# DeltaNet and SwiGLU on one Trainium2 core: gate and value of the late chunks by 15 block products for 18

## The chip, the core and the metric

The kernel runs on one core of a Trainium2 chip. A core has five engines that run side by side, each in the order of its own queue: TensorE (PE in the profile, its weight loads PEld) multiplies matrices into PSUM, VectorE (DVE) does elementwise work and 32x32 transposes, ScalarE (ACT) applies functions and copies, GpSimd (POOL) does elementwise work in SBUF, and SyncE (SP) issues transfers. They wait for each other by semaphores. The metric is the device time of one launch in microseconds; smaller is better.

## The reference

Two blocks follow each other. The first is a delta rule: for each of 4 x 8 heads a 48x48 state is carried over 768 positions. The second is a feed-forward block on the result, with 3072 tokens of 384 numbers (8 heads x 48) and 1536 hidden ones.

```python
k_n = k / (np.linalg.norm(k, axis=-1, keepdims=True) + 1e-06)
for t in range(S):
    y[:, :, t] = q_t @ state
    v_old = state^T @ k_t
    state = state + beta_t * outer(k_t, v_t - v_old)
...
g = x @ w_gate
silu = g * (1.0 / (1.0 + np.exp(-g)))
val = x @ w_val
return (silu * val) @ w_out
```

All inputs and outputs are float32.

## The kernel before, in words

The 768 positions are cut into 12 chunks of 64; a chunk is 256 tokens of the feed-forward block (4 batches x 64 positions), held transposed as `x_ffn`, three row blocks of 128 by 256 tokens. Two chunks make a group, whose triangular systems are inverted together.

**Recurrence.** `advance(c)` takes chunk c through four steps, each a few bundles of 64 small matmuls with VectorE or ScalarE in between. Step 1: products of keys and queries with the state (L924 into bank pair `px`, L933 into `py`), and the values minus the first (L941). Step 2: the inverse applied (L963) and copied (L975). Step 3: the new state (L1031, L1040), the output y (L1019) and its three copies (L1076, L1078). Step 4: y transposed (L1092) and copied to `x_ffn` (L1098).

**Preparation.** Keys and queries of later chunks are transposed (`turned`, L494: one operation of VectorE for a chunk's keys, one for its queries) and multiplied (`gram_steps`, L521). `invert(g)` then inverts the systems of group g. It is a generator: transposes (L563), norms and a power on GpSimd (L826), 31 pairs of a multiplication and an addition for the forward substitution (L593, L599; on VectorE for group 1, on GpSimd from group 2 on), transposes back (L563, L858, L863) and four copies of ScalarE (L869). It yields a cost after each piece, and the word `WAIT` where time is to pass. `fill(n)` runs it until costs of n are spent or until a `WAIT`. `join(g)` completes the inverse by two bundles of matmuls (L887, L901) with a copy of ScalarE between; for group 1 the joins are `join_late` (L792, L804).

**The order.** The engines' orders are as written (`manual_schedule`). `point(c)` places the next step of `advance(c)`, or a step of preparation; `finish(c)` places all that are left.

**Chunks 0 and 1** run their gate and value plainly (`gate_val`, L1295) while the weights are loaded and converted, then their outputs (`output`, L1322), in the order (0,0), (0,1), (1,0), (1,1). In `output(1, 1)` VectorE also makes sums of weight blocks (`sums_of_w`, 24 operations of 128x256, up to 175 us), nine of which are stored to DRAM (`kept`). GpSimd's last work before it is a memset of the `qpad` tiles (L158) at 121.84 to 123.68.

**Chunks 2 to 11** work in three rounds (`gate_val_fast`). A round treats two pairs of hidden blocks, f1 and f2, for gate and value and both halves of the tokens. Plainly that is 12 products of a weight block pair with an x block; a scheme of sums of blocks (as in Strassen's method) does it with 11. One product is `product4`: four matmuls of a 128x128 weight block with 128 tokens, each of which shows as two records, all on line L1199. ScalarE copies partial results from one PSUM bank to another (L1212, L1255) or to SBUF (L1252), VectorE adds them (`plus`, L1366; `minus` is L1363), ScalarE takes the silu of the gate half of a bank (L1229), and VectorE multiplies it by the value half (L1234) into `h_f`. Three of the summed weights are streamed from DRAM in each round (L1226). Recurrence and preparation lie at points within the rounds, with calls of `fill`, 12 a chunk with those of the output.

**Output of these chunks** (`output_fast`) is seven products of six matmuls of 128x192 (L1405, twelve records a product) on sums of h made by VectorE.

PSUM has eight banks: four `ffn_banks`, and the pairs `px` and `py`. The function `product4` and the round's beginning are:

```python
def product4(p, w, moving, start=False):
    for u in range(4):
        nc.tensor.matmul(
            p[:, u], w(u), moving, start=start and u == 0, stop=True,
            skip_group_check=True,
        )
```

Of the kernel before, what the change touches and what calls it, by code (L numbers as in the profile page):

```python
# [20 lines left out]
def kernel(  # L21
# [42 lines left out]
    ffn_pool = ctx.enter_context(tc.tile_pool(name="ffn", bufs=2))  # L64
# [129 lines left out]
    wg_sb = const.tile([128, KT, DFF], FP32, name="wg_sb")  # L194
    wv_sb = const.tile([128, KT, DFF], FP32, name="wv_sb")
# [5 lines left out]
    for f0, m in ((0, 256), (256, 256), (512, 256), (768, 256), (1024, PIECE)):  # L201
        for t in range(KT):
            for dst, src in ((wg_sb, moe_w_gate), (wv_sb, moe_w_val)):
                pieces.append((dst, src, t, f0, m))
    N_HALF = sum(piece[4] < PIECE for piece in pieces)
# [58 lines left out]
    def power_step(n):  # L264
        if n in powers or n not in staged:
# [7 lines left out]
            dst[:, t, f0 : f0 + m],  # L273
            words_of[:, :, 1].bitcast(FP32),
# [5 lines left out]
    def convert(ns, ahead=6):  # L280

        work_of = []
        for n in ns:
            dst, _, t, f0, m = pieces[n]
            power_step(n)
            place = staged.pop(n)[:, 0:m]
            work_of.append((dst[:, t, f0 : f0 + m].bitcast(U32), place, powers.pop(n)))
# [59 lines left out]
    kt, qt, a_sb, a_of, p_sb, xts = {}, {}, {}, {}, {}, {}  # L347

# [563 lines left out]
    def advance(c):  # L912
# [169 lines left out]
        xts[c] = ffn_pool.tile([128, KT, TOK], FP32, name="x_ffn")  # L1082
# [38 lines left out]
    def w_s(n, c):  # L1121
        if n < 4:
            return units(hp[5 + n])
        return units(hp[10] if c == FAST else p_places[0][:, 0:512])

    def m5_of(c, r):
        early = c == FAST and r == 0
        return units(hp[13] if early else p_places[0][:, 512:1024])

    kept = {  # L1130
        (n, r): dram.tile([128, 4, 128], FP32, name=f"w_s{n}_{r}")
        for n in (1, 2, 4)
        for r in range(3)
    }
    x_t = const.tile([128, 3, 128], FP32, name="x_t")

    def w_pair(m, t, f):
        return (wg_sb, wv_sb)[m][:, t, 128 * f : 128 * f + 256].rearrange(
            "p (i n) -> p i n", i=2
        )  # L1140

    made_in = {
        0: {1: hp[6], 2: hp[7], 4: hp[10]},
        1: {1: hp[1], 2: hp[2], 4: hp[0]},
        2: {1: hp[12], 2: hp[13], 4: hp[8]},
    }

    def sum_of_w(n, r):

        f1, f2 = 2 * r, 2 * r + 6  # L1150
        for m in range(2):
            s1, s2, s4 = (units(made_in[r][k])[:, 2 * m : 2 * m + 2] for k in (1, 2, 4))
            if n == 1:
                plus(s1, w_pair(m, 0, f2), w_pair(m, 1, f2))
            elif n == 2:
                minus(s2, s1, w_pair(m, 0, f1))
            elif n == 4:
                minus(s4, w_pair(m, 1, f1), s2)
            else:
                minus(w_pair(m, 0, f2), w_pair(m, 0, f1), w_pair(m, 0, f2))  # L1160
        if n != 3:
            nc.sync.dma_start(out=kept[n, r], in_=units(made_in[r][n]))

    sums_at = {
        2: [(1, 1), (2, 1), (4, 1)],
        4: [(1, 2), (2, 2), (4, 2)],
        6: [(3, 1), (3, 2)],
        8: [(1, 0), (2, 0)],
        12: [(4, 0), (3, 0)],
    }  # L1170

    def sums_of_w(f):
        for job in sums_at.pop(f, ()):
            sum_of_w(*job)

    def sums_of_x(c):

        left, right = slice(0, 128), slice(128, 256)
        b1, b2 = xts[c][:, 0], xts[c][:, 1]
        minus(x_t[:, 0], b1[:, right], b1[:, left])  # L1180
        minus(x_t[:, 1], b2[:, right], x_t[:, 0])
        minus(b1[:, right], b2[:, right], b1[:, right])
        minus(x_t[:, 2], b2[:, left], x_t[:, 1])
# [8 lines left out]
    ROUNDS = 3  # L1192

    p_x, p_w, p_y, p_v = (units(bank) for bank in ffn_banks)
    tok = slice(0, 128), slice(128, 256)

    def product4(p, w, moving, start=False):
        for u in range(4):
            nc.tensor.matmul(  # L1199
                p[:, u], w(u), moving, start=start and u == 0, stop=True,  # L1200
                skip_group_check=True,
            )

    def plain(t, f):
        return lambda u: w_pair(u // 2, t, f)[:, u % 2]

    def summed_w(n, c):
        return lambda u: w_s(n, c)[:, u]

    def begin(c, r):  # L1210
        product4(p_x, plain(0, 2 * r), xts[c][:, 0, tok[0]], True)
        nc.scalar.copy(p_y, p_x)  # L1212
# [5 lines left out]
    def gate_val_fast(c, r, fill):  # L1218

        f1, f2 = 2 * r, 2 * r + 6  # L1220
        x, m5 = xts[c], m5_of(c, r)

        def next_sums(n):
            to = c + (r == ROUNDS - 1)
            if to < NCH:
                nc.sync.dma_start(out=w_s(n, to), in_=kept[n, (r + 1) % ROUNDS])  # L1226

        def silu(p, n):
            nc.scalar.activation(  # L1229
                sil[:, n].rearrange("p (i n) -> p i n", i=2), p[:, 0:2], ACTF.Silu  # L1230
            )

        def times(p, n, f, j):
            nc.vector.tensor_tensor(  # L1234
                out=h_of(c, f, j),
                in0=sil[:, n].rearrange("p (i n) -> p i n", i=2),
                in1=p[:, 2:4],
                op=ALU.mult,
            )

        more = 1.5 if (c, r) <= (FAST + 1, 0) else 0

        def combo_and_fill(n):
            if c == FAST:
                combos.pop(0)()
                n -= 1.9
            fill(n)

        for f in (f1, f2):
            new_h(c, f, f // 2)  # L1250
        product4(p_w, summed_w(1, c), x_t[:, 0], True)
        nc.scalar.copy(m5, p_w)  # L1252
        next_sums(1)
        product4(p_y, summed_w(2, c), x_t[:, 1])
        nc.scalar.copy(p_v, p_y)  # L1255
        next_sums(2)
        load_late()
        product4(p_x, plain(1, f1), x[:, 1, tok[0]])
        product4(p_x, plain(2, f1), x[:, 2, tok[0]])
        plus(p_y, p_y, m5)  # L1260
        product4(p_v, plain(0, f2), x[:, 0, tok[1]])
        silu(p_x, 0)
        fill(1)
        times(p_x, 0, f1, 0)
        plus(p_w, p_v, m5)
        point_and_fill(c + 1, 3.4 + more, fill)
        product4(p_y, summed_w(4, c), x[:, 1, tok[1]])
        next_sums(4)
        load_late()
        product4(p_y, plain(2, f1), x[:, 2, tok[1]])  # L1270
        silu(p_y, 1)
        times(p_y, 1, f1, 1)
        product4(p_w, plain(2, f2), x[:, 2, tok[1]])
        silu(p_w, 0)
        times(p_w, 0, f2, 1)
        product4(p_v, plain(1, f2), x_t[:, 2])
        product4(p_v, plain(2, f2), x[:, 2, tok[0]])
        silu(p_v, 1)
        sums_of_h(c, f2)
        times(p_v, 1, f2, 0)  # L1280
        if r < ROUNDS - 1:
            begin(c, r + 1)
        else:
            clear(0)
# [521 lines left out]
```

## Time and profile before

| what | value |
|---|---|
| median of 3 runs | 699.82 us (698.36 to 700.54) |
| the profiled execution's own time | 696.37 us |
| its span, first to last instruction | 694.7 us |
| TensorE busy | 681.7 us (98%) |
| VectorE busy | 411.2 us (59%) |
| ScalarE busy | 259.5 us (37%) |
| GpSimd busy | 192.3 us (28%) |
| mean granted clock of TensorE | 0.994 |
| chunk 2 begins | 172 us |
| records of gate and value, chunks 2 to 11 (L1199) | 2640 |

The profile is of one execution. Its page lists the busy time of each engine, the span in 40 slices, the DMA queues, the chain of work that ended last, and the costliest groups of instructions. A row of the groups names the line, the engine, the operation, what it writes and reads, how often it ran, then its busy time and the mean duration of one in ns, then the idle time of the engine ahead of it and what ended that. The answers of the trace show the same execution further: the chain in order of time (start, duration, what), the timeline (start, duration, engine, line, operation) and a table of busy times in stretches, whose last three columns are TensorE's granted clock, the busy share of the DMA engines and GB/s. Times in such answers count from the span's start.

### The profile page before, as it was taken

Reading aid. Unit: us, or ns where it says so; the run is one execution under the profiler, and the core shown is the slowest. Engines: PE = TensorE matmul, PEld = TensorE weight load, DVE = VectorE, ACT = ScalarE, POOL = GpSimd, SP = SyncE. Lnnn points to the kernel's source line nnn. Section 1 sums busy time; section 2 is a strip of 40 time slices with the busy share of each in tenths; the row PEclk is TensorE's granted clock in tenths of the full one; section 3 lists DMA queues with packets and bytes.
Section 4 is the critical chain, followed back from the end, with each engine's and each line's share of the span. In section 5 each row is a group of like instructions: output and inputs, shape, how many; then the busy total and the mean of one; then the engine's idle time right before and its main releaser. Section 6 shows DMA issues by size and latency. Waiting matters only on the chain.

```text
span 694.7 us, 25664 instructions
## 1 busy us (share of the span) xinstructions
PE 681.7 (98%) x11380; PEld 636.3 (92%) x11380; DVE 411.2 (59%) x856; ACT 259.5 (37%) x549; POOL 192.3 (28%) x310
## 2 busy tenths in 40 slices
PE   8899999999999999999999999999999999999997
PEld 4688888757999999999999999999999999999997
DVE  6886789798657755647446456455565345333342
ACT  4774876214442532344233244233143242142230
POOL 5010031106882128820038820328800000000000
PEclk9899999999999999999999999999999999999999
DMA  9578724017550621464423363233363221121210
GB/s 137 151 187 215 215 78 151 1 35 177 128 111 14 116 79 40 105 119 79 93 72 70 74 134 70 56 84 72 67 119 70 56 63 46 55 63 46 69 47 23
DMA packets 143854, 62.31 MB, mean 90 GB/s; under 512 B 122976, under 2 KB 126048, under 8 KB 143744
## 3 DMA queue, kind: packets, MB, share of 16 engines
q1 hardware_dynamic: 141536, 60.19, 37.1%
q8 instruction: 89, 1.46, 0.9%
q10 hardware_dynamic: 2080, 0.39, 0.4%
q0 software_dynamic: 128, 0.10, 0.1%
q14 instruction: 21, 0.17, 0.1%
HBM read 53.58 MB, written 7.08 MB: 87 GB/s over the span
## 4 chain that ended last, share of the span: by engine, by line
PE 96%; ACT 2%; issue 1%; DVE 1%; DVEq 0%; ACTq 0%
PE ffn L1199 43%; PE ffn L1405 20%; PE ffn L1295 9%; PE ffn L1322 4%; PE p_px L963 2%; PE p_px L924 2%; PE p_py L933 2%; PE p_px L1031 1%; PE p_py L521 1%; PE p_py L1019 1%; PE p_px L521 1%; PE p_py L1092 1%; PE ffn L983 1%; PE p_px L645 1%; PE p_px L983 1%
## 5 line engine op out<-in xcount | busy, mean ns | idle before, releaser
L1199 PE MATMUL ffn<-x_ffn,wg_sb 128*128 128x128 f32 x840 | 128.2, 275 | 0.2 <-ACT x_ffn L1098 0.2
L1199 PE MATMUL ffn<-x_ffn,wv_sb 128*128 128x128 f32 x840 | 128.1, 275 | 0.0
L1199 PEld LDWEIGHTS ffn<-x_ffn,wg_sb 128*128 128x128 f32 x840 | 111.1, 192 | 0.3 <-ACT x_ffn L1098 0.3
L1199 PEld LDWEIGHTS ffn<-x_ffn,wv_sb 128*128 128x128 f32 x840 | 110.7, 192 | 0.0
L1234 DVE TENSOR_TENSOR h_f<-sil,ffn 128x256 f32<-128x256 f32 x120 | 49.9, 417 | 78.2 <-ACT sil L1229 76.4
L1229 ACT ACTIVATE sil<-ffn 128x256 f32<-128x256 f32 x120 | 46.1, 384 | 132.5 <-PE ffn L1199 130.8
L1405 PE MATMUL ffn<-wo_sb,h_f 128*128 128x192 f32 x480 | 83.4, 327 | 0.0
L826 POOL TENSOR_TENSOR n_b<-mb,half 128x32 f32<-128x32 f32 x5 | 30.0, 6003 | 183.3 <-DVE mb L563 183.3
L1366 DVE TENSOR_TENSOR ffn<-ffn,p_sb 128x512 f32<-128x512 f32 x58 | 40.5, 698 | 64.1 <-ACT ffn L1255 62.8
L1405 PEld LDWEIGHTS ffn<-wo_sb,h_f 128*128 128x128 f32 x480 | 78.1, 190 | 0.4
L599 POOL TENSOR_TENSOR zb<-zb,tmp 128x31 f32<-128x31 f32 (+15 forms) x124 | 71.4, 576 | 9.7
L593 POOL TENSOR_TENSOR tmp<-zb,mb 128x31 f32<-128x31 f32 (+15 forms) x124 | 67.0, 541 | 16.0 <-DVE mb L580 6.6
L1199 PE MATMUL ffn<-x_t,h_f 128*128 128x128 f32 x480 | 61.0, 280 | 0.2 <-ACT ffn L1212 0.2
L1199 PEld LDWEIGHTS ffn<-x_t,h_f 128*128 128x128 f32 x480 | 56.2, 191 | 1.4 <-ACT ffn L1212 0.4
L1366 DVE TENSOR_TENSOR o_sb<-o_sb,ffn 128x192 f32<-128x192 f32 x49 | 17.2, 352 | 61.9 <-PE ffn L1405 60.7
L1212 ACT COPY ffn<-ffn 128x512 f32<-128x512 f32 x30 | 17.1, 571 | 63.9 <-PE ffn L1199 63.9
L1405 PE MATMUL ffn<-last_k,h_f 128*128 128x192 f32 x200 | 35.9, 327 | 0.0
L1363 DVE TENSOR_TENSOR h_f<-h_f,h_f 128x256 f32<-128x256 f32 x60 | 30.2, 512 | 9.2 <-PE ffn L1405 8.2
L1295 PE MATMUL ffn<-x_ffn,wg_sb 128*128 128x256 f32 x144 | 34.4, 385 | 0.0
L1295 PE MATMUL ffn<-x_ffn,wv_sb 128*128 128x256 f32 x144 | 33.8, 382 | 0.0
L1405 PEld LDWEIGHTS ffn<-last_k,h_f 128*128 128x128 f32 x200 | 32.9, 190 | 0.0
L1295 PEld LDWEIGHTS ffn<-x_ffn,wg_sb 128*128 128x128 f32 x144 | 26.5, 190 | 4.4 <-DVE wg_sb L309 0.8
(304 smaller groups left out, 1100.2 us busy)
## 6 DMA issues: line engine op xcount, KB each, us to landing
h_f<-w_s SPq DMA_DIRECT2D x60, 256.0 KB, 2.8
p_sb<-w_s SPq DMA_DIRECT2D x27, 256.0 KB, 2.6
vin<-in_v_dram SPq DMA_DIRECT2D x48, 96.0 KB, 3.1
out_dram<-o_sb SPq DMA_DIRECT2D x48, 96.0 KB, 2.2
kn<-in_k_dram SPq DMA_DIRECT2D x20, 192.0 KB, 4.5
zt<-in_moe_w_out_dram SPq DMA_DIRECT2D x6, 384.0 KB, 3.6
qpad<-in_q_dram SPq DMA_DIRECT2D x36, 64.0 KB, 3.3
w_s<-h_f SPq DMA_DIRECT2D x7, 256.0 KB, 4.0
```

What stands on the lines that cost most here:

```text
L593: engine.tensor_tensor(out=t_v, in0=zb[:, 0 : j + 1, j : j + 1].to_broadcast([128, j + 1, m]), in1=mb[:, j : j + 1, j + 1 : R].to_broadcas ...
L599: engine.tensor_tensor(out=zb[:, 0 : j + 1, j + 1 : R], in0=zb[:, 0 : j + 1, j + 1 : R], in1=t_v, op=ALU.add,)
L826: nc.gpsimd.tensor_tensor(out=n, in0=mb.rearrange("p j i -> p (j i)")[:, 0 : R * R : R + 1], in1=half, op=ALU.pow,)
L1199: nc.tensor.matmul(p[:, u], w(u), moving, start=start and u == 0, stop=True, skip_group_check=True,)
L1212: nc.scalar.copy(p_y, p_x)
L1229: nc.scalar.activation(sil[:, n].rearrange("p (i n) -> p i n", i=2), p[:, 0:2], ACTF.Silu)
L1234: nc.vector.tensor_tensor(out=h_of(c, f, j), in0=sil[:, n].rearrange("p (i n) -> p i n", i=2), in1=p[:, 2:4], op=ALU.mult,)
L1295: nc.tensor.matmul(ps[name][:, i], w_sb[:, t, (f + i) * 128 : (f + i + 1) * 128], xts[c][:, t], start=(t == 0 and i == 0), stop=(t == KT - 1),
L1322: nc.tensor.matmul(p_o, hs[c, f - f % 2][:, f % 2, bp * 128 : (bp + 1) * 128], wo_sb[:, f], start=(f == 0), stop=(f == FT - 1),)
L1363: nc.vector.tensor_tensor(out=out, in0=a, in1=b, op=ALU.subtract)
L1366: nc.vector.tensor_tensor(out=out, in0=a, in1=b, op=ALU.add)
L1405: nc.tensor.matmul(p[x, part], a(f - f % 2)[:, f % 2], b(f), start=not begun and f == 0, stop=f == FH - 1, skip_group_check=True,)
```

## The change

Chunks 2 to 11 work in two halves instead of three rounds. A half (`r`) treats three pairs of hidden blocks, `PAIRS[r]`, for gate and value and both token halves: plainly 18 products, here 15. The order of its products and of the work on their banks is a list, `STEPS`, written out for both halves: `P` is a product into a bank (with a start flag where it is 1), `C` a copy from a bank to another with or without a minus sign, `T` a copy to an SBUF tile, `A` an addition or subtraction of such a tile, `S` a silu, `M` the multiplication. Five banks are used: the four `ffn_banks` (0 is `ffn2`, 1 `ffn3`, 2 `ffn0`, 4 `ffn1`) and the second bank of `px` (3).

VectorE makes ten sums of x blocks a chunk (`X_SUMS`, 128x128 each) instead of four operations. Gate and value weights move to one tile `w_all`, so that a pair's gate and value blocks lie together, 512 wide. The weight sums (`W_SUMS`, 16 for each half, 128x512 each) are made once by GpSimd, issued in the outputs of chunks 0 and 1 by `w_step`, many of them in place; six a half are stored to DRAM and streamed in each chunk through three tiles (`STREAM`, 12 loads a chunk for nine).

The steps of `advance(c + 1)` and the preparation move from the rounds into `output_fast`: `visit` places a step of the recurrence, and first completes the inverse and the joins that it needs; `prep_turn`, `prep_gram` and `prep_join` place the parts of the preparation. Within the halves remain two calls of `fill(1)` (after the first and the seventh operation of VectorE in the first half; in chunk 2 the sums of output weights instead), late loads, possible joins, and sums of h. Two calls of `fill` stand at the end of an output. Chunk 3's keys and queries and the last two joins of group 1 are placed ahead of chunk 2.

```diff
+    X_SUMS = (
+        (6, 0, 1, 1, -1), (7, 4, 1, 6, -1), (8, 5, 1, 7, -1),
...
+    W_SUMS = (
+        (9, 1, 1, 2, 1), (1, 2, 1, 5, 1), (10, 6, 1, 1, 1),
...
+    STREAM = (-1, -1, 5, 3, 1, -1, 4, 0, -1, 2, -1, -1, -1, -1, -1)
+    PAIRS = ((3, 1, 0), (2, 5, 4))
+    STEPS = (
+        ("P", 2, 10, 1),
+        ("P", 3, 7, 1),
+        ("C", 2, 0, -1),
+        ("P", 4, 5, 1),
+        ("P", 0, 4, 0),
...
+        ("T", 1, 1, 0),
+        ("A", 4, 1, 1),
+        ("P", 1, 11, 0),
+        ("S", 3, 2, 0),
+        ("P", 4, 2, 0),
+        ("M", 3, 2, 0),
+        ("S", 1, 0, 0),
+        ("M", 1, 0, 0),
+        ("T", 4, 0, 0),
+        ("S", 4, 1, 0),
+        ("A", 2, 0, 1),
+        ("S", 2, 4, 0),
+        ("M", 4, 1, 0),
+        ("M", 2, 4, 0),
+    )
...
-    def gate_val_fast(c, r, fill):
+    def gate_val_fast(c, r, behind):
+        for kind, a, b, s in STEPS:
+            bank = g_banks[a]
+            if kind == "P":
+                i = STREAM[b]
+                w = streams[i % 3] if i >= 0 else w_home(r, W_OF[b])
+                product4(bank, w, x_place(X_OF[b]), s > 0)
+                if i >= 0:
+                    load_stream(c, r, i + 3)
...
@@ def output(c, bp, fill, between=())
             if f in between:
                 fill(2)
                 point(2)
-                if (c, bp) == (1, 1):
-                    sums_of_w(f)
+            w_step(W_PACE)
...
+    def visit(c, fill):
+        n = c + 1
+        if n == NCH:
+            return
+        while not may_advance(n):
+            fill_some(1000)
+            prep_step(c)
+        step("advance", advance, n)
...
@@ def output_fast(c, fill)
+        visit(c, fill)
+        for f in (2, 4):
+            first_sums(c, f)
+        product_1()
         if c > FAST:
             clear(1)
+            visit(c, fill)
+            for f in (2, 4):
+                last_sum(c, f)
             product_2()
+            plus(o[0][:, right], o[0][:, right], p[0, 1])
+            visit(c, fill)
+            prep_turn(c)
             product_3()
             plus(o[1][:, right], o[0][:, right], p[1, 0])
+            visit(c, fill)
+            x_sums(c + 1)
             product_4()
+            prep_gram()
...
@@ the loop over chunks
         for c in range(2, NCH):
+            some = [lambda: fill(1)]
...
+                (0, "D", 1): some,
+                (0, "D", 7): some,
...
+            for r in range(2):
+                gate_val_fast(c, r, behind)
             output_fast(c, fill)
-            finish(c + 1)
-            x_sums(c + 1)
```

## The prediction

> **What bounds the kernel now.** I read four views: busy shares and chain, the chain in order of time, the groups, then timelines.
>
> ```profile
> PE 681.7 (98%) x11380; PEld 636.3 (92%) x11380; DVE 411.2 (59%) x856; ACT 259.5 (37%) x549; POOL 192.3 (28%) x310
> ...
> PE 96%; ACT 2%; issue 1%; DVE 1%; DVEq 0%; ACTq 0%
> ```
>
> TensorE is the chain, and from 174 us on it has almost no hole. So work taken off it is a gain, and each new wait of it is a loss. The chain in order of time prices both kinds of work in chunk 11, where nothing is mixed in:
>
> ```profile
> 647.36 29.57 PE ffn L1199 x264
> 676.93 13.67 PE ffn L1405 x84
> ```
>
> 264 records are 33 block products of eight: 0.896 us a product. One of the seven output products is 13.67/7 = 1.95 us. The groups (last number ahead of the second bar: mean ns) price what hangs behind TensorE:
>
> ```profile
> L1234 DVE TENSOR_TENSOR h_f<-sil,ffn 128x256 f32<-128x256 f32 x120 | 49.9, 417 | 78.2 <-ACT sil L1229 76.4
> ...
> L1366 DVE TENSOR_TENSOR ffn<-ffn,p_sb 128x512 f32<-128x512 f32 x58 | 40.5, 698 | 64.1 <-ACT ffn L1255 62.8
> ...
> L1252 ACT COPY p_sb<-ffn 128x512 f32<-128x512 f32 x29 | 17.0, 586 | 24.5 <-PE ffn L1199 24.2
> ...
> L563 DVE STREAM_TRANSPOSE zt<-zb 128x512 f32<-128x512 f32 x8 | 9.6, 1202 | 0.0
> ...
> L869 ACT COPY zt<-zt 32x512 f32<-32x512 f32 x16 | 9.2, 610 | 0.1
> ...
> L863 DVE STREAM_TRANSPOSE z<-zt 32x256 f32<-32x256 f32 x16 | 6.1, 415 | 0.2
> ```
>
> A silu (L1229) is 0.38 us. The timeline gives the hand-overs: the load after a product starts at 395.27, the silu of that product at 395.58 (0.31 us), its multiplication 0.04 us after the silu's end; ScalarE to TensorE takes 0.05 us (174.20 to 174.25). Last, GpSimd beside VectorE, and the join that waits for the inverse of group 1:
>
> ```profile
> 154.52 0.75 PE L792 MATMUL p_px<-zt,a_sb 32*32 32x32 f32 x64
> ...
> 279.70 0.64 POOL L593 TENSOR_TENSOR tmp<-zb,mb 128x256 f32<-128x256 f32 x1
> 279.73 0.76 DVE L1363 TENSOR_TENSOR x_t<-x_ffn 128x128 f32<-128x128 f32 x1
> 280.42 0.73 POOL L599 TENSOR_TENSOR zb<-zb,tmp 128x256 f32<-128x256 f32 x1
> 280.52 0.77 DVE L1363 TENSOR_TENSOR x_t<-x_ffn,x_t 128x128 f32<-128x128 f32 x1
> ...
> 438.74 0.28 DVE L1363 TENSOR_TENSOR x_t<-x_ffn 128x128 f32<-128x128 f32 x1
> ```
>
> The same subtraction takes 0.28 us alone and 0.76 beside GpSimd: each time it ends 0.15 us after GpSimd's operation does (280.34 and 280.49; 281.15 and 281.29). It stood still until GpSimd was through.
>
> **The change, part by part.**
>
> *Products.* 30 for 33 in each of ten chunks: 30 x 0.896 = 26.9 us less. There is no other saving: TensorE's other work stays.
>
> *Between the two halves of a chunk.* After the last product (P 4,2) bank 2 still waits for T 4, A 2, S 2 and M 2, and the next half opens with P 2,10 into that bank. TensorE takes its queue in order. 0.31 + 0.59 (copy) + 0.03 + 0.70 (sum) + 0.03 + 0.38 (silu) + 0.03 + 0.42 (product) + 0.05 = 2.54 us idle; ten times, 25.4. Before, the next round's first bank had been read long ago. Inside a half I walked all 15 products at 0.896: the copies end 0.02 to 0.07 us late at four places, 0.2 us a half. Bounds over 20 halves: 0 (hand-overs a little quicker) and 10 (0.3 more where a fill of 1.2 us stands ahead of A 4,1); I take 2.
>
> *Into the output.* The same tail covers bank 2, where product 1 begins. The first step of the recurrence stands between (L924 and L933, 1.08 + 0.93 us): 0.55 us is left, for chunks 2, 4, 6, 8, 10: 2.7. Chunk 11 has no recurrence: 2.5. Further on I find no wait: each of the four steps has a product of 1.95 us behind it against 0.95 (subtraction) or 1.43 (three y copies); the ten sums of x at 0.28 end some 6 us before they are read. The clears (0.33) and all the sums of h keep ahead of their products.
>
> *The inverses.* An inverse is fed by calls of fill, and has 28 steps, 15 of which only pass a turn. Before there were 12 calls a chunk, so an inverse took two chunks. Now there are four (after D 1 and D 7, and two at the output's end), some nine steps in two chunks. So at the outputs of chunks 3, 5, 7, 9 the visit finds the inverse unfinished, and its loop issues the rest there, ahead of the recurrence and of product 1. Walk, from the last product's end: VectorE is free at 2.5; two transposes to 4.9; join on TensorE 5.0 to 6.2; six z1 transposes to 7.2; ScalarE's four copies to 7.3 and the join's factor to 7.9; second join 7.9 to 9.1; recurrence; its second half waits for the join's copies (VectorE has two transposes of the next inverse first) to 10.9; product 1 at 11.8. Of this 4.4 is work that existed: 7.4 idle, four times 29.6. GpSimd's substitution (38.4 us, 260.9 to 299.3) starts a chunk of some 50 us earlier and is done. Bounds: 0.55 (the tail already done) and 9 (a transfer late too); the walk's own rows decide.
>
> *Weight sums.* 24 sums at 0.42 leave VectorE, at 154 to 175, where TensorE idled 0.6 us in all: worth 0 to 0.6, taken as 0. 32 sums of 128x512 go to GpSimd. Its rows go from 0.25 us (31 elements) to 0.67 (255): 1.15 us at 512. They are ready to run at 122, where GpSimd is free; 25 stand ahead of the two memsets of qpad, 29 ahead of the power for group 2. From 124.3 to 151.3 VectorE runs 62 steps of the inverse of group 1, both operands in SBUF, each needing the one before. By the rows above each waits out the sum in flight, one for one: 27 sums x 1.15 = 31 us later, and L792, then the rest of output(1,1), is queued behind it with 1 us of slack: 30. Bounds: 0 (no hindrance) and 36 (all 32). I take 30, by the nearest rows. The power then comes late as well, but the join is later still. Moving chunk 3's q and k and two joins ahead of chunk 2 adds a wait for two transposes: 1, between 0 and 6.
>
> The Trainium skill, "SBUF — State Buffer", section "Who interferes with whom", says that a VectorE instruction with two SBUF inputs and a GpSimd instruction that reads SBUF exclude each other for the whole instruction; the two rows agree, so by that rule too the term is 30 and not 0.
>
> *Transfers.* SP gets 12 stream loads a chunk for 9, each 2.8 us to landing, with 5.2 us of eight block loads queued ahead at two places; the tightest (first load of the second half) lands about when it is read. 0 to 1 us a chunk; I take 0.
>
> *Clock.* Where TensorE idled 1.29 us between one-column matmuls, its clock halved (third number from the end):
>
> ```profile
> 27.16 0.97 PE L652 MATMUL p_px<-half 32*32 32x1 f32 x96 [1.29 <-issue]
> ...
> 28.00:30.00 2.00, 2.00 (x16) 0.54 (x6) 1.97 (x4) 0.96 (x2) 0.18 (x1) 0.50 0.45 132
> 30.00:32.00 2.00, 2.00 (x92) 1.94 (x91) 2.00 (x5) 0.08 (x1) 0.18 (x1) 0.64 0.48 138
> ```
>
> That is 2 x 0.50 + 2 x 0.36 = 1.7 us lost. I charge it to the five long holes (four visits, the join): 8.5. The ten holes of 2.5 us have full matmuls on both sides, unlike this row: 0 to 17, taken as 0.
>
> The Trainium skill, "TensorE: Matmul & The Clock Gate", Part 1, says that the clock halves after an idle window of about 3.4 us; by that only the long holes count, and the row with 1.29 us speaks against it.
>
> **Sum,** against the profiled execution (span 694.7, its time 696.4; the median of the runs, 699.8, stands 3.4 above, which I don't add): -26.9 + 25.4 + 2 + 2.7 + 2.5 + 29.6 + 30 + 1 + 8.5 = +74.8, so 771.
>
> **The rivals.**
> *GpSimd's sums hinder nobody* (VectorE gets in between as a rule, or the sums run elsewhere): 771 - 30 - 1.7 = 739. For it: VectorE got two subtractions through between two GpSimd operations at 281.2. Against: those were independent of each other.
> *The inverse's tail holds nobody,* because it is issued in time: 771 - 4 x 6.9 - 6.8 = 737; with the former too, 705. Against: the count of calls.
> *Short holes halve the clock too*: 771 + 17 = 788, by the row above.
> *Faster:* TensorE does not stand behind its own queue, since what is issued is reordered and ready products fill the holes: only the saving is left with some 3 us of prologue, 672. It decides if the new idle of TensorE stays under 26.9 us in all, 2.7 a chunk. Against it: the timeline of before shows the written order everywhere.
>
> **How the numbers follow.** Likeliest, all walks right: 0.50, 750 to 795 by the bounds of its terms. Sums harmless 0.19; tail harmless 0.09; both 0.05; short holes 0.06; faster 0.11. Range 703 to 795: it leaves out the faster case and some of the edges. About 0.3% is what a measurement of this kernel can tell from no change; no case lies within it but the edges, 0.02, taken from the faster side and the two milder ones: faster 0.10, slower 0.88.
>
> **What would show it.** Ten holes of 2.5 us in TensorE between the halves, ended by VectorE's multiplication (1, 2 or 5 us elsewhere would be wrong); holes of some 5 us at the outputs of chunks 3, 5, 7, 9 ended by L563; substitution rows of VectorE above 1 us from 124 on and L792 near 184; a product still at 0.9 us. The prediction is wrong if the fast stage's TensorE has no holes, or chunk 2 begins before 180.

## The result, and the profile after

The changed kernel takes 804.61 us (median of 4 runs, 800.96 to 809.94), the one before 700.18 beside it: 1.150 times as long, 95% interval 1.141 to 1.158. The prediction said 771 (703 to 795): the direction is right, the size is not. The profiled execution took 801.51 us, its span is 799.8, so 105.1 above the span of before, where 74.8 was forecast.

The first row of the page of the changed kernel, the busy time of each engine:

```profile
PE 701.3 (88%) x11140; PEld 646.0 (81%) x11140; DVE 497.5 (62%) x974; ACT 323.7 (40%) x659; POOL 233.0 (29%) x342
```

TensorE went from 98% busy to 88%, with 240 records fewer: it now waits. Its mean granted clock is 0.921, where it was 0.994. The waits of TensorE in the changed kernel (line, what was waited for, us in total, how often, longest):

```profile
PE ffn L1301 <- DVE h_f L1342: 22.9, 10, 2.4
PE p_px L811 <- issue: 22.4, 1, 22.4
PE p_px L906 <- DVE zt L582: 18.1, 4, 4.5
...
PE p_px L1301 <- DMA h_f<-w_s: 2.6, 3, 1.7
PE ffn L1301 <- DMA p_sb<-w_s: 2.1, 3, 1.4
```

The first three rows are the prediction's places: ten holes between the halves (L1301 is the block product, L1342 VectorE's multiplication), the join that waits for the inverse of group 1 (L811), and four visits that find an inverse unfinished (L906 is the first join of a group). For L811 the profile names no releaser ("issue"); the last operation of that inverse, L787, ends 0.1 us before it. The last two are stream loads that came late, which the prediction took as 0.

One hole in the chain in order of time, of chunk 10:

```profile
712.49 0.59 ACT p_sb L1332
...
713.11 0.71 DVE ffn L1433
...
713.84 0.39 ACT sil L1337
...
714.26 0.43 DVE h_f L1342
...
714.74 1.47 PE ffn L1301 x8
```

Copy, sum, silu, multiplication: these are the four steps of the prediction's walk, 2.47 us from TensorE's last product to its next. What the walk left out is in the last row: the eight records of one product take 1.47 us where 0.9 was usual. The table of stretches shows it in chunk 11 (columns: stretch, length, then busy time and instructions of PE, PEld, DVE, ACT and POOL, then TensorE's granted clock, the DMA share, GB/s): first half, hole, second half.

```profile
749.03:762.80 13.77, 13.77 (x122) 13.71 (x121) 6.06 (x11) 6.80 (x13) 0.00 (x0) 1.00 0.43 112
762.80:765.28 2.48, 0.20 (x3) 0.01 (x2) 1.62 (x4) 1.26 (x3) 0.00 (x0) 1.00 0.55 173
765.28:780.63 15.35, 15.35 (x120) 15.29 (x121) 6.73 (x13) 7.02 (x14) 0.00 (x0) 0.89 0.18 53
```

The same 15 products take 13.77 us ahead of the hole and 15.35 behind it, at a mean clock of 0.89. In eight of the ten chunks (not 4 and 9) a stretch of 3.41 us at half clock follows the hole (6.83 in chunk 2).

Why eight and not ten is in the trace too. The stretches at half clock begin whole multiples of 3.41 us apart (at 227.32, 288.76, 408.23 and 476.49, for example: 18, 35 and 20 such intervals), so the span falls into fixed intervals of that length. In the table of stretches, the interval with most of chunk 8's hole and the one behind it, then the interval with most of chunk 9's hole:

```profile
592.55:595.96 3.41, 1.39 (x11) 1.00 (x9) 2.15 (x6) 1.64 (x4) 2.78 (x9) 1.00 0.76 93
595.96:599.37 3.41, 2.99 (x14) 2.99 (x15) 0.36 (x1) 0.58 (x1) 2.94 (x7) 0.50 0.56 211
...
647.16:650.57 3.41, 1.51 (x13) 1.51 (x14) 1.44 (x3) 1.23 (x4) 0.00 (x0) 1.00 0.89 241
```

TensorE idles 2.02 us of the first, and the next is at half clock; it idles 1.90 of the last, since the rest of that hole lies in the interval before, and no half clock follows. The same was counted in the changed kernel and in the four runs below that keep these ten holes (weight sums that read nothing, the sums later, TensorE kept busy in the visits, the inverse issued in time): 31 holes left TensorE 1.91 us or more of idle time in one interval (a wait for a load in the same interval included), and half clock followed all of them; 19 left 1.90 or less, and it followed none. How a hole falls differs from run to run: in those four, five or six of ten were followed.

Chunk 2 starts at 207.8 (172.0 before) and the last product ends at 795.4. So of the 105.1 us, 35.8 lie ahead of chunk 2 and 69 behind. VectorE and GpSimd in the timeline, within the inverse of group 1, and its end:

```profile
139.55 1.27 POOL L1229 TENSOR_TENSOR w_all<-w_all 128x512 f32<-128x512 f32 x1
139.68 1.33 DVE L612 TENSOR_TENSOR tmp<-zb,mb 128x175 f32<-128x175 f32 x1
...
176.60 2.17 DVE L787 STREAM_TRANSPOSE zt<-zb 128x1024 f32<-128x1024 f32 x1
```

The step of VectorE ends 0.19 us after GpSimd's sum; 28 of its 62 steps look like this, and the transposes behind them (L787) start at 176.6 instead of 151.3. The visits, last, in the same table of stretches, from the last product of a half to output product 1: chunk 7, which is visited with an unfinished inverse, then chunk 4, which is not.

```profile
545.48:560.00 14.52, 8.32 (x386) 7.58 (x385) 11.01 (x18) 5.12 (x9) 5.28 (x1) 0.59 0.12 33
...
368.59:370.72 2.13, 2.13 (x130) 1.96 (x128) 1.32 (x4) 1.26 (x3) 1.89 (x4) 1.00 0.52 164
```

It is 14.5 us for 2.1, at a clock of 0.59; the rest of the output takes 19.7 and 19.8. From the end of a chunk's gate and value to the next chunk the four visits take 34.8, 36.6, 34.2 and 35.7, chunk 4 takes 21.9. Less 2.44 us a visit for the work of the two joins, 44.0 us are lost in all.

### The profile page after: what moved, and what is told of

Same layout as the page of the kernel before. It is cut to its first block, busy times and chain, and to the rows that moved or that the text cites. A ratio compares the mean times of both kernels' runs of the same rounds, so it can differ in the third digit from the quotient of the medians.

```text
span 799.8 us, 25628 instructions
## 1 busy us (share of the span) xinstructions
PE 701.3 (88%) x11140; PEld 646.0 (81%) x11140; DVE 497.5 (62%) x974; ACT 323.7 (40%) x659; POOL 233.0 (29%) x342
## 5 line engine op out<-in xcount | busy, mean ns | idle before, releaser
L1301 PE MATMUL ffn<-x_ffn,w_all 128*128 128x128 f32 x1440 | 192.0, 285 | 23.3 <-DVE h_f L1342 22.9
L1301 PEld LDWEIGHTS ffn<-x_ffn,w_all 128*128 128x128 f32 x1440 | 179.6, 199 | 26.2 <-DVE h_f L1342 22.2
L1332 ACT COPY p_sb<-ffn 128x512 f32<-128x512 f32 x80 | 46.9, 586 | 64.4 <-PE ffn L1301 64.0
L1361 PE MATMUL ffn<-x_ffn,w_all 128*128 128x256 f32 x288 | 65.4, 383 | 0.0
L1361 PEld LDWEIGHTS ffn<-x_ffn,w_all 128*128 128x128 f32 x288 | 53.7, 190 | 7.8 <-DVE w_all L324 0.4
L1433 DVE TENSOR_TENSOR o_sb<-o_sb,ffn 128x192 f32<-128x192 f32 x51 | 17.7, 349 | 57.9 <-PE ffn L1489 32.7
L1301 PE MATMUL p_px<-x_ffn,h_f 128*128 128x128 f32 x320 | 49.2, 304 | 2.6 <-DMA h_f<-w_s 2.6
L1342 DVE TENSOR_TENSOR h_f<-sil,ffn 128x256 f32<-128x256 f32 x80 | 33.5, 419 | 28.8 <-ACT sil L1337 26.0
L1301 PEld LDWEIGHTS p_px<-x_ffn,h_f 128*128 128x128 f32 x320 | 45.3, 218 | 3.1 <-DMA h_f<-w_s 3.1
L1301 PE MATMUL ffn<-x_ffn,h_f 128*128 128x128 f32 x320 | 45.5, 286 | 0.0
L1301 PE MATMUL ffn<-x_ffn,p_sb 128*128 128x128 f32 x320 | 42.8, 277 | 2.6 <-DMA p_sb<-w_s 2.1
L1332 ACT COPY h_f<-ffn 128x512 f32<-128x512 f32 x60 | 35.2, 586 | 17.3 <-PE ffn L1301 14.7
L1301 PEld LDWEIGHTS ffn<-x_ffn,p_sb 128*128 128x128 f32 x320 | 38.9, 192 | 3.7 <-DVE h_f L1342 2.0
```

The source lines that it names most:

```text
L1301: nc.tensor.matmul(units(p)[:, u], units(w)[:, u], moving, start=start and u == 0, stop=True, skip_group_check=True,)
L1332: nc.scalar.copy(temps[b], bank)
L1342: nc.vector.tensor_tensor(out=h_of(c, f, b // 3), in0=sil_of[b], in1=units(bank)[:, 2:4], op=ALU.mult,)
L1361: nc.tensor.matmul(ps[name][:, i], w_cols(n, t, f + i), xts[c][:, t], start=(t == 0 and i == 0), stop=(t == KT - 1), skip_group_check=True,)
L1433: nc.vector.tensor_tensor(out=out, in0=a, in1=b, op=ALU.add)
```

## The experiments

Each is an edit of the changed kernel, so 804.6 us is what it is compared with; the kernel before, run beside them, took 698.1 to 698.7. The fast stage is the time from chunk 2's first product to the end of the last product's weight load: 587.3 us in the changed kernel's profile, 518.2 before.

### Weight sums that read nothing

```diff
-                signed_sum(nc.gpsimd, place(out), place(a), sign_a, place(b), sign_b)
+                for _ in range(2):
+                    nc.gpsimd.memset(place(out), 0.0)
```

> Each of GpSimd's 32 weight sums is replaced by two memsets of the same place, so GpSimd stays busy over the same stretch but reads nothing from SBUF; the weight sums are left out of the computation. Theory (VectorE's two-operand work in SBUF stands still while GpSimd reads SBUF): VectorE's rows of the inverse of group 1 go from 1.2 to 1.4 us back to 0.42, L787 from 176.6 back to near 152, chunk 2's first product from 207.8 to 176 to 183 (172 of before, plus the 3.9 us of moved preparation, plus its waits), the time from 804.6 to about 777 (772 to 783). Rival (GpSimd is only late with the power and the memsets that others wait for): chunk 2 stays at 203 to 208, the time at 799 to 806.

Measured: 778.03 us (775.28 to 779.27). GpSimd and VectorE in that profile:

```profile
138.63 2.15 POOL L1279 MEMSET p_sb<- 128x512 f32 x4
139.06 0.41 DVE L612 TENSOR_TENSOR tmp<-zb,mb 128x240 f32<-128x240 f32 x1
...
154.84 2.26 DVE L787 STREAM_TRANSPOSE zt<-zb 128x1024 f32<-128x1024 f32 x1
```

GpSimd is nearly as busy as before (a pair of memsets takes 1.1 us, a sum took 1.3), VectorE's steps are back at 0.41 us, and L787 starts 21.8 us earlier. So it is the reading and not the business of GpSimd that holds VectorE. Chunk 2 starts at 186.7, not at 176 to 183 as expected. Of the 14.6 us that remain to before, 3.5 are there at L787 already (the inverse takes its 27.0 us as before, but starts that much later); the others lie between the last step of the recurrence (L1111, 174.07) and the first product, where the moved preparation waits for itself: transposes, the products of keys and of queries one after the other, their copies, VectorE's mask behind ten sums of x, the join.

### The sums later

The first half's sums are issued in the second half of chunk 1's last output, the second half's in chunk 2, and the scaling of group 2 waits for them:

```diff
+        while g == 2 and not w_done:
+            yield WAIT
...
-            w_step(W_PACE)
+            if (c, bp) == (1, 1) and f >= 6:
+                w_some(3)
...
+            if c == FAST:
+                behind[0, "P", 8] = [w_rest]
```

> GpSimd's weight sums start only behind the inverse of group 1 and the power for group 2: those of the first half in the last output of chunk 1, those of the second half during the first half of chunk 2, the substitution of group 2 behind them. Nothing is left out. Theory (what costs is the alternation with VectorE's chain of two-operand work): the inverse of group 1 ends near 157, chunk 2 starts at 188 to 196 where it was 207.8, the time falls from 804.6 to about 789 (784 to 794). Rival (the sums only collide elsewhere, with the sums of x and the second half of chunk 2, whose stores come late): 797 to 806.

Measured: 796.37 us (794.42 to 797.98), between the two ranges and next to the rival's. The inverse is in time (L787 at 155.64) and chunk 2 starts at 192.4, but the collision went elsewhere. The timeline of VectorE in this run, then two of TensorE's waits:

```profile
178.51 6.55 DVE L1231 TENSOR_TENSOR x_ffn<-x_ffn,x_ffn 128x128 f32<-128x128 f32 x5
```

```profile
PE p_py L823 <- DVE p_sb L558: 9.0, 1, 9.0
PE p_px L1318 <- DMA h_f<-w_s: 7.7, 2, 7.2
```

A sum of x now takes 1.3 us instead of 0.28, the join waits 9.0 us behind them, and the second half of chunk 2 waits 7.2 us for a sum that GpSimd has made late and that has to go to DRAM and back.

### TensorE kept busy in the holes

```diff
             for r in range(2):
                 gate_val_fast(c, r, behind)
+                if r == 0:
+                    for n in (512, 512, 256):
+                        nc.tensor.matmul(pairs_of_banks["px"][:, 0, 0:n], ident,
+                                         w_home(0, 0)[:, 0:n], start=True, stop=True)
```

> Three unread matmuls (512, 512 and 256 columns, some 2.2 us) are put into each hole between the halves; nothing is left out. The hole stays as long, but TensorE works in it. Theory (a hole of 2.5 us is enough to halve the clock): no window at half clock behind the holes, second halves go from 154.1 us in sum to 141 to 143, the time from 804.6 to about 792 (789 to 795). Rival (the second halves are slow for their late stream loads or other waits): 802 to 807, second halves still near 154.

Measured: 790.98 us (789.71 to 795.64), 13.6 less. Chunk 11 again, the hole and the second half in stretches as above:

```profile
758.55:761.02 2.47, 2.35 (x8) 0.99 (x7) 1.62 (x4) 1.25 (x3) 0.00 (x0) 1.00 0.57 174
761.02:774.75 13.73, 13.72 (x120) 13.67 (x121) 6.72 (x13) 7.02 (x14) 0.00 (x0) 1.00 0.19 59
```

The hole is as long, but with 2.35 us of unread products in it the half behind it takes 13.73 instead of 15.35. All ten second halves lie between 13.72 and 13.87 (sum 137.5; it was 154.1, some 4 of it late loads), and no half clock follows any hole. So the half clock came of the idle time in the hole.

### Another bank first

```diff
-            bank = g_banks[a]
+            bank = banks_of[a]    # g_banks, in the second half g_banks in the order (2, 4, 0, 3, 1)
...
-        p = {(0, part): ps_ffn([128, DH], "p_o", 2 + part) for part in range(2)}
+        p = {(0, part): ps_ffn([128, DH], "p_o", part) for part in range(2)}
```

> The second half of a chunk takes the five banks in another order, so that its first product goes into a bank that was read long ago; the bank still under work is then needed by a copy two products later. Theory (bank 2 alone makes the hole, and its idleness the half clock behind it): the ten holes of 2.5 us shrink to about 0.5 (-20), and the eight windows at half clock behind them go too (-13): 804.6 to about 772 (767 to 778). Rival A (the half clock comes from elsewhere): -20, 785. Rival B (the tail only moves, the copy into the busy bank now holds TensorE): 798 to 805.

Measured: 792.79 us (792.42 to 793.04). (In this order of the banks a copied partial result is lost where the output has begun a bank, so part of the sums is left out of the values; the instructions and their operands' sizes are the same.) The holes are gone, to 0.1 us, and another wait stands behind them. From the waits of TensorE, then from SyncE's timeline between the halves of chunk 4:

```profile
PE p_px L1301 <- DMA h_f<-w_s: 19.0, 9, 3.1
```

```profile
350.00 4.47 SPq L172 DMA_DIRECT2D qpad<-in_k_dram  x8
354.57 0.91 SPq L1297 DMA_DIRECT2D h_f<-w_s  x2
```

The second product of a half reads the first stream load, and that load is issued at 354.57, behind eight block loads. The hole of 2.5 us had been hiding it. None of the three expectations is met as written: 25 us of holes went, 16 us of load waits came.

### Another bank first, and the loads moved

The same with an order that keeps the output's banks, (2, 1, 0, 3, 4), and with the block loads taken out of the middle of the halves:

```diff
-                (0, "P", 2): late,
-                (0, "P", 6): late + join_some,
-                (0, "P", 10): late,
+                (0, "P", 2): late + late,
+                (0, "P", 6): join_some,
...
             product_4()
+            load_late()
             prep_gram()
```

> The second half takes the banks in another order again (first product into a bank long read, the busy one is third), and the block loads of keys and queries leave the place in each half where the stream loads for the next half are queued behind them. Nothing is left out. Theory (the hole of 2.5 us hid the stream load that the block loads hold up; with both mended nothing is left to wait for but 0.3 to 0.5 us): the ten holes and the half clock behind them go, the waits for stream loads too: 804.6 to about 769 (765 to 775). Rival (the stream loads are late by their own duration and not by the queue): the second product of each second half still waits 2 us, 785 to 793.

Measured: 782.15 us (779.12 to 790.47), between the two ranges, for a reason that neither names. No second half waits for a load any more: they take 14.26 to 14.33 us each. The waits are in the first halves now (14.6 to 19.8 us in chunks 2 to 9, where 13.78 is free of them), because the block loads, moved to the end of the output and the first half's start, stand ahead of other stream loads there:

```profile
PE p_px L1301 <- DMA h_f<-w_s: 13.8, 7, 4.3
```

In chunks 10 and 11, which have no block loads, both halves are free of it (13.78 and 14.26). So the queue and not the load's own duration is what is late.

### TensorE kept busy in the visits

Four unread matmuls of 512 columns ahead of the first join of a visit, one ahead of the second:

```diff
         while not may_advance(n):
             fill_some(1000)
+            if n // 2 in inverted:
+                for _ in range(4 if steps("join", n // 2) == 0 else 1):
+                    nc.tensor.matmul(pairs_of_banks["px"][:, 0], ident,
+                                     w_home(0, 0), start=True, stop=True)
             prep_step(c)
```

> At the visits that find the inverse unfinished (outputs of chunks 3, 5, 7, 9) four unread matmuls of 512 columns, some 3.6 us, stand ahead of the first join, where TensorE waits 4.5 us for the transposes, and one ahead of the second. Nothing is left out. Theory (part of a visit's 11 us is the half clock, which lasts 13.65 us behind the wait): the windows at half clock at the four visits go or shrink to one, each of these outputs is 4 to 5 us shorter, the time falls from 804.6 to about 787 (783 to 791). Rival (the joins and the recurrence are slow there for other waits, and the clock only follows): 800 to 806.

Measured: 800.36 us (795.16 to 803.26). The visit of chunk 7, from the last product to output product 1, in the table of stretches:

```profile
538.93:553.85 14.92, 11.77 (x397) 8.42 (x395) 11.02 (x18) 5.12 (x9) 5.66 (x2) 0.79 0.08 24
```

The clock rises from 0.59 to 0.79 and the visit is no shorter, 14.92 for 14.52. The four take 34.7, 34.0, 35.6 and 35.6 us now, 1.3 less in all, which is the rival's result. It does not settle what the clock is worth. The edit brings the first join of every visit from 1.9 to 1.29 us, but the step behind it waits for ScalarE's four copies, which in the changed kernel too end 0.25 us behind that join. The second join starts 1.1 to 2.0 us later than before, behind its unread matmul, and still takes 1.8 to 1.9 us. So the half clock of the first join costs next to nothing; what it costs from the second join on is not shown.

### The inverse issued in time

```diff
-        for _ in range({1: 2, 2: 3}.get(g, 4)):
+        for _ in range({2: 3}.get(g, 2)):
...
-            for _ in range(11):
+            for _ in range(2 if g == 2 else 4):
...
-            some = [lambda: fill(1)]
+            some = [lambda: fill(6)]
```

> The fills within the halves run more of the inverse, and it passes fewer turns, so that it is through, and the joins fall, before the outputs of chunks 3, 5, 7, 9. Nothing is left out. Theory (the visits' unfinished inverse costs 11 us each in waits and half clock): those four outputs go from 34 to 37 us to 22 to 25, some 2 to 3 us each come back as a stall in a half where VectorE's transposes stand ahead of a sum: -32 to -44, so 760 to 773. Rival (the wait goes with the work: VectorE's 4.7 us of transposes hold the products of a half as long): 792 to 805.

Measured: 789.96 us (786.04 to 791.41), just under the rival's range and far from the theory's. The visits are mended: the four outputs take 20.9 to 21.9 us from half to next chunk. The halves pay for it, as the waits of TensorE show:

```profile
PE ffn L1301 <- ACT h_f L1332: 13.5, 12, 1.5
PE ffn L1301 <- DVE ffn L1430: 8.3, 7, 1.3
```

Neither wait is in the changed kernel, nor a third of 5.7 us behind ScalarE's copies to SBUF. A first half takes 16.1 or 18.0 us instead of 13.8 to 14.3, a second half with joins 19.5 to 22.7. So both are true: an unfinished inverse costs 11 us a visit, and two thirds of that are paid again where it is issued, since a half has no room for an operation of 1.2 us on VectorE or 0.6 on ScalarE.

### The inverse at the ends of outputs

```diff
-            some = [lambda: fill(1)]
+            some = [lambda: fill(1000)]    # runs to the next WAIT; an inverse has one after each of five pieces
...
             store(c, 1, o[1])
-            fill(2)
-            prep_join(c)
+            fill(1000)
             product_7()
...
-                nc.scalar.copy(z[:, :, 0:R], z[:, :, R:C])
+                nc.gpsimd.tensor_copy(z[:, :, 0:R], z[:, :, R:C])
...
                 gate_val_fast(c, r, behind)
+                if r == 0 and c > FAST:
+                    prep_join(c)
```

> The inverse is cut into five pieces: its first transposes at the end of an output, norms and scaling in the next half, the transposes back at the end of the next output, the last transposes in the half after it; four copies go from ScalarE to GpSimd; the first join stands in the hole between the halves of chunks 3, 5, 7, 9 and the second at the entry of their outputs. Nothing is left out. Theory (an inverse in time costs little if its VectorE work lies at the ends of outputs, where VectorE has some 3 us free): the outputs of chunks 3, 5, 7, 9 go from 35 us to 23 or 24, their halves stay within 2 us of the others: 804.6 to about 765 (760 to 771). Rival (each piece in a half costs TensorE its whole duration, 4.9 us of VectorE's for a group): 780 to 788.

Measured: 775.97 us (774.00 to 779.10), 28.6 less, between the two. The four outputs with what precedes them take 27.2, 27.1, 27.0 and 25.8 us, 34 less than in the changed kernel. Nine come back in the first halves: 16.15 us in even chunks (norms and scaling, 2.4 us), 14.6 to 15.7 in odd ones.

### All of it, with and without the sums

The second order of the banks, the inverse at the ends of outputs, and every block load in the output ahead of product 4 (in chunk 2 they stand behind the second product):

```diff
             x_sums(c + 1)
+            while late_loads:
+                load_late()
             product_4()
```

> The other order of the banks and the inverse in five pieces together, and all block loads (values, keys, queries) now stand in the outputs, where no stream load is queued behind them. Nothing is left out. Theory (holes, visits and late loads are separate costs and add): the fast stage, 587.7 us in the changed kernel, 571.4 with the banks and 561.2 with the inverse mended alone, goes to about 537 (-16.4, -26.5, -13 for the loads, +5 for four joins that stood in a hole), the time to about 754 (748 to 761). Rival (the hole also gave ScalarE and VectorE time to catch up, so that the pieces of the inverse cost more without it): 764 to 776.

Measured: 758.82 us (755.47 to 762.97), as expected. The fast stage is 541.6 us (537 expected): 15.9 and 26.1 less for the two parts alone, 45.7 together. So the gains from the holes and from the visits add; what the loads bring beside them is 3.7 us, where 8 were expected (13 less 5 for the joins). Six us of the stage are one wait for a stream load in chunk 2, whose first half still holds block loads.

> As the run before it, and each of GpSimd's weight sums replaced by two memsets, so the weight sums are left out of the computation. It bounds what a better place for the sums could give at most. Theory (the prologue's cost is the alternation and is separate from the stage behind it): 26 us less than the run before it, about 728 (720 to 736), which is still above the 699 of the kernel before. Rival (without the late start the stage behind loses as much elsewhere, as the substitution of group 2 starts no earlier): 740 to 755.

Measured: 734.82 us (732.15 to 737.11), 24.0 less, ratio to before 1.054 (1.049 to 1.058). Chunk 2 starts at 185.4, and the fast stage takes the same 541.9 us. The memsets hold GpSimd nearly as long as the sums did, so this is no strict bound for the prologue. But even with the prologue of the kernel before, a fast stage of 541.9 us for 518.2 leaves that run 24 us longer, so no better place for the sums alone would make it the faster one. Chunk 11, where no recurrence and no preparation is left, says why in small. Second half and output of the run with the sums, in the table of stretches (its first half takes 13.78); then products and output of the kernel before:

```profile
721.88:736.15 14.27, 14.20 (x123) 13.82 (x121) 8.42 (x17) 8.05 (x16) 0.00 (x0) 1.00 0.29 85
737.53:752.05 14.52, 13.89 (x84) 13.59 (x84) 5.52 (x16) 1.25 (x4) 0.00 (x0) 1.00 0.01 1
```

```profile
647.04:676.74 29.70, 29.70 (x266) 29.70 (x266) 12.15 (x26) 9.40 (x20) 0.00 (x0) 1.00 0.24 67
676.66:690.28 13.62, 13.62 (x87) 13.62 (x85) 3.77 (x10) 1.47 (x5) 0.00 (x0) 1.00 0.00 1
```

Thirty products take 28.0 us, 1.7 less than 33 did; 1.4 are lost between them and the output, and 0.9 within it. The chunk is 43.9 us against 43.2. So in this chunk, with the hole mended, what three products save is spent by the waits that are left.

## Why the prediction was right in kind and short in size

By the spans, in us; the measured column is read from the two profiles, the products by their count, the half clock from the second halves and the run with busy holes:

| term | forecast | measured |
|---|---|---|
| 300 products for 330 | -26.9 | -26.9 |
| ten holes between halves | +25.4 | +24.8 |
| half clock behind them | 0 | about +12 |
| waits within halves | +2 | +8.5 |
| stream loads | 0 | +4.7 |
| into and within the outputs, chunk 11 included | +5.2 | +3.4 |
| four visits with their clock | 29.6 + 6.8 | +44.0 |
| prologue: inverse of group 1, moved preparation, clock | 30 + 1 + 1.7 | +31.9 |
| not placed | | about +3 |
| sum | +74.8 | +105.1 |

**The step that failed is the clock of the short holes, "taken as 0".** The prediction had the row that spoke (1.29 us idle, then half clock) and set it aside because that row stood between one-column matmuls. The holes stand between full matmuls, and eight of ten halved the clock: about 1.5 us each. The run with busy holes shows the cause, 13.6 us in medians. "Short holes halve the clock too" was a rival with a chance of 0.06; it is the one that happened, for 12 of its 17 us. The prediction gave every short hole or none the half clock; the trace gives it to a hole that leaves 1.91 us of idle time in one interval of 3.41. This is the largest part of the 30.3 us that were missing, but alone it would have left the time at 783, within the range: the visits (7.6 short), the waits within halves (6.5) and the loads (4.7) did the rest.

The Trainium skill, "TensorE: Matmul & The Clock Gate", Part 1, names a free-running window of 3413 ns, and the stretches at half clock here are indeed 3.41 us or multiples of it; but it asks for an idle window, and here 1.91 us of idle time in a window of 3.41 were enough, so the measurement decides against weighing by that rule.

**The visits** are where they were forecast, four of them, ended by L582 (L563 of before). The term is 7.6 us short. The walk put product 1 at 11.8 us after the last product; it came at 14.5 in chunk 7. The joins took 1.93 and 2.24 us there instead of 1.22, the second part of the recurrence's first step 2.0 instead of 0.93, and the join's two last copies, taken as side by side, ran one after the other, 1.0 us more. The joins and the recurrence ran at half clock here. The run with busy visits lifted it for the first join alone and gained next to nothing by that, so how much of the 7.6 us is the clock's stays open.

**Into the outputs** 5.2 us were forecast, and none came there: product 1 begins in `ffn2`, which is bank 0 of `STEPS`, and not in the bank 2 that the prediction named. Instead one product of chunk 2's output waits 2.8 us for differences of h that stand behind the sums of x on VectorE, and one of chunk 11's waits 0.6 us for a clear.

**Waits within halves**: 13.78 us where nothing else stands in a half, so 0.34 a half and not 0.1; and 0.43 more in four halves where a piece of the inverse stands ahead of a sum. My walk had 0.2 a half, and I took half of it.

**Transfers**, taken as 0: late loads cost 4.7 us, and the first run with another bank shows that the holes hid some 16 more (19.0 of waits for 2.6). The step "5.2 us of eight block loads queued ahead" was right, and I weighed it against a second half that started 2.5 us late.

**The prologue** came out (31.9 for 32.7) in part by luck, since its parts are off both ways. L787 is 25.3 us late and the join behind it (L811) 24.4, where 30 was forecast. Of the 25.3 the run with memsets gives 21.8 back: 28 steps of VectorE wait out a sum, 27 were forecast, but each loses some 0.95 us and not 1.15. That GpSimd's memsets hinder nobody also agrees with the Trainium skill, "SBUF — State Buffer", "Who interferes with whom", by which a GpSimd instruction that reads SBUF holds such an operation of VectorE and one that only writes doesn't. The moved preparation, put at 1, costs 4.8 us of idle time here (from L1111 at 195.85 to the first product at 207.83 it is 10.2 us more than before: 3.9 are the moved work, and the 1.5 left are put down to half clock from 200.01 to 203.42 and from 206.84 on), and nearly 7 in the run with memsets. The other 1.2 us lie in the last output of chunk 1: the clock was at half for 23.9 us, from 159.05, within the long wait, to 182.95, 4.1 us behind it.

Right were the holes' place, length and last releaser, the visits' number and place, the alternation, and that nothing else pays for 240 records fewer. The rivals "sums hinder nobody", "the tail hinders nobody" and "faster" are refuted by the rows above.

## What to carry to other kernels

Fewer products are a gain only while the engine has the next one ready: here three products in 33 were worth 2.7 us a chunk, and one dependence at the seam of two halves cost 2.5 plus, in eight of ten, some 1.5 for the clock behind it. When a hole is closed, ask what it was hiding: here a load queue (16 us) and, in chunk 11, 1.4 us of work of ScalarE ahead of the output. And price an idle gap of TensorE by the idle time within one interval that halved the clock in the trace; here, between full matmuls, that was 1.91 us.

## What the runs showed of the hardware

- Holes of 2.47 us between full matmuls were followed by half clock in eight of ten cases, 3.41 us of it in seven and 6.83 in one, and in five or six of ten in four other runs with the same holes; waits of about 2 to 3 us for loads, in the run with the first other order of banks, in three of eight.
- Half clock began on fixed intervals of 3.41 us. It followed all of 31 holes that left TensorE idle for 1.91 us or more of one interval, and none of 19 that left it idle for 1.90 or less.
- With matmuls in 2.35 of the 2.47 us, none of ten was.
- VectorE's operations with both operands in SBUF ran at full speed (0.41 us) beside GpSimd's memsets and at 1.3 us beside its sums, here for the inverse's steps and, with the sums later, for the sums of x (0.28 alone).
- A visit with small bundles and waits stayed at half clock for 13.65 us in three of four cases and 17.07 in the other.
